# Three of the eight operations that decode a piece of weights go to ScalarE and GpSimd, the triangular solves are shared out anew, and the whole order is written again

## The chip, the cores and the metric

The kernel runs on one core of a Trainium2 chip. A core has a matrix engine (TensorE, PE in the profile, its weight loads PEld), a vector engine (VectorE, DVE), a scalar engine (ScalarE, ACT), GpSimd (POOL), and SyncE (SP), which here only issues DMAs. Each engine works through its own queue in order; semaphores tie the queues together. The metric is the device time of one launch in microseconds, as the median of several runs, in float32.

## The reference

A linear attention with decay and a delta rule runs over 768 time steps, for 4 batches and 8 heads of width 40. Its output, as 320 features for each token, goes through a gated feed-forward layer with a three-tap convolution along time.

```python
for t in range(S):
    y[:, :, t] = einsum('bhd,bhde->bhe', rt, state)
    Sa = einsum('bhde,bhe->bhd', state, at)
    state = state * wt[:, :, None, :] - einsum('bhd,bhe->bhde', Sa, bt) \
          + einsum('bhd,bhe->bhde', vt, kt)
# x = y, heads side by side: (4, 768, 320)
h = maximum(x @ w_in, 0)                       # 320 -> 1024
conv_out[s] = sum_k conv_w[k] * h[s + k - 1]   # along the tokens
return (h * sigmoid(conv_out)) @ w_out         # 1024 -> 320
```

The three weight arrays `w_in`, `conv_w` and `w_out` arrive as float64 and are read as pairs of 32-bit words. The kernel makes float32 numbers of them with integer and float operations (`from_f64`), and then a high and a low part of each, for products in several passes.

## The kernel before, in words

**Attention** goes in 24 steps of 32 tokens, two steps to a pair (12 pairs, `j` = 0 to 11). For a pair: `decays` (cumulated products of the decay, L365 to L381), `decayed` (a, k and b times these, L391 and L399), `scores` (`at`, L437: the products of the chunk), and from `at` the right-hand side `bb`, which goes through DRAM (`bd`) to bring one small triangular system to each partition (L461, L465). `solve` (L471 to L498) inverts them in 31 rounds of a multiply (L480) and an add (L486) and sends the result `xx` through DRAM (`xd`, L491) back to `tt` (L496). `VSOL` names the pairs whose solve is done by VectorE; the others are done by GpSimd. There is one buffer each for `xx`, `bb` and the temporary.

`chain` is the recurrence from step to step: `pp` on TensorE (L514, L522), its copy `psb` on ScalarE (L527), `pu` on TensorE from `psb` and `tt` (L533), its copy `u` (L538), the update `pn` on TensorE (L549), the addition of the old state on VectorE (`s`, L562), and its decay on GpSimd (`s`, L568), four instructions each for four batches. Both steps of a pair need `tt`, so steps 2j and 2j+1 can't end before solve j. Then `pairs`, `outputs` and `finish` give the 320 features of the step (`xf` L657, `xh` L665, `xl` L667).

**The feed-forward layer** goes in 12 windows of 64 tokens (two steps each): `moe_in` in four parts of 256 hidden columns (L700 to L743: products, relu, the taps L721 and L729, sigmoid L734, gating L736, split into high and low, L740 and L743), and `moe_out` in two halves (L754, L771).

**The weights** come in 23 pieces, 12 of `w_in` (`wi`), one of `conv_w` (`cv`) and 10 of `w_out` (`wo`, `wp`). A piece is a DMA, `from_f64` (eight VectorE operations of 128 x 256, L217 to L235), a cast to the high part on ScalarE (L253) and the low part on GpSimd (L255). The buffers of the pieces (tags `gh` and `gl`, four each) are those that the gated products of `moe_in` use later, so the first products wait for the last pieces.

**What sets the order.** Nothing is scheduled at run time: `ORDER` is a written list of tokens, such as `ch2*2`, and each token advances one generator to its next `yield`. Every instruction goes into its engine's queue in that order. A token that isn't ready in the sense of `put` first advances what it needs. Semaphores only make an engine wait at the head of its queue.

Of the kernel before, what the change touches and what calls it, by code (L numbers as in the profile page):

```python
# [8 lines left out]
F32 = mybir.dt.float32  # L9
# [11 lines left out]
VSOL = range(0, 12, 2)  # L21
# [13 lines left out]
    ld0 de0.0*2 ld0*2 de0.1 ld0 ld1 de0.1 we0 dd0.0*3 dd0.1*2 sc0 dd0.1 we0 ld1*2 lr0 sc0 sc1 lr1  # L35
    de1.0 sc1 ha0 de1.0 dd1.0 de1.1*2 we1*4 si0 ha0 ha1 dd1.0 we0*2 rt0 ld1 so0 ha1 dd1.0 so0 dd1.1
    ld2 so0*2 ld2 dd1.1 ld2 so0 dd1.1 ha2*2 sc2 ld2 lv0 lv1 vt0 ha3*2 so0*3 sc2 sc3 we2*2 sc3 we3
    we2*2 we3 we4 so0 we3*2 we5 we4 we5 si1 de2.0*2 ch0*4 we4*2 we6 lv2 de2.1*2 so1*2 ld3 ut0 pa0
    vt1 dd2.0*2 de3.0 we5 so1 we5 we7 ou0 we6 fi0 so1 dd2.0 ch1 we6 dd2.1 we7*2 ch1 we7 dd2.1*2 ld3
    st1*2 sc4 we6 so1 we8*4 we9 we10 ch1 lv3 rt1 we9 st1*2 ut1 pa1 lr2 ou1 ha4 ld3*2 we10 so1*3 fi0  # L40
    vt2 we10 fi0 fi1 de3.0 sc4 sc5 we9 we10 sc5 ch1 de3.1 we9 de3.1 ha4 we11 we12 lr3 rt2 fi1 st2*2
    fi1 we11 we12 we11*2 ro0 we13 we12*2 ha5 st2 we13 we14 ha5 ld4 so1 we13 dd3.0*3 dd3.1*3 we14*2
    ch2 si2 so2 ch2 pk0 ut2 so2*2 pa2 vt3 sc6 so2*2 st2 ou2 ch2 ro0 rt3 mi0.0*3 so2*2 mi0.0*2 ch2
    st3*2 we13 mi0.1*2 st3 ld4 so2 ld4 we14 lv4 we15 we16 ch3*2 sc6 sc7 ut3 we15 st3 we15 sc7 fi2*3
    lr4 mi0.0 pa3 mi0.0 ch3 we15 ch3 we16 mi0.0 we17 mi0.1 mi0.2 we17*2 mi0.2 so2 ch4 si3 we16 so3
    ou3 ha6 we16 we18 de4.0 we18 ha6 ha7 st4 fi3*2 we17 we19 de4.0 we18 mi0.1 we19 vt4 st4*3 lv5
    de4.1 ch4 ut4 so3 ch4 dd4.0 rt4 we18 we20 de4.1 we20 mi0.2 so3 we20 pa4 vt5 ch4 ch5 so3 mi0.2
    ch5 fi3 ha7 we19*2 we21*2 ut5 we20 we22*2 ou4 st5*2 mi0.1 st5 lr5 rt5 so3 we22 ld4 ld5 de5.0
    mi0.1 we21 ch5 we22 mi0.3 we21 mi0.0*2 so3 mi0.1*2 mi0.3 pa5 mi0.3 pk1 dd4.0*2 dd4.1 mi0.1*2
    dd4.1 st5 mi0.2 sc8 fi4*2 ld5 dd4.1 ou5 mi0.2 lv6 mi0.3 so3*2 sc8 mi0.2 sc9 mi0.2*2 ha8*2 ha9  # L50
    fi4 fi5 ld5 de5.0 de5.1 ha9 sc9 mi0.2 dd5.0 mi0.3 dd5.0 de5.1 lv7 mi1.0*3 mi1.1 ld5 dd5.0 dd5.1
    sc10 so3 si4 mi0.3 lr6 dd5.1*2 ch5 mi0.3 lr7 mi0.3 mi1.1*2 mi1.0*3 mi1.1 mi1.2 vt6 sc10 mi0.3
    mo0.0 sc11 mi0.3 mi1.1 mi1.0*2 mi1.1 ch6 st6 mi1.2 ch6*2 sc11 mi1.1*2 mo0.0*2 ch6 mo0.0 mo0.1*5
    ld6 ut6 rt6 ch7 mi1.1 so4 ld6 so4*2 pa6 vt7 st6 fi5*2 st6 so4*2 mi1.0 so4 mi1.2 st6 mi1.3 so4
    mi1.2 so4 lv8 ou6 mi1.0 mo1.0 mi1.2 mi1.3*2 st7*2 ch7 ut7 mi1.1 st7*2 rt7 ch7*2 mo1.0 pa7
    mi1.3*2 fi6*2 pk2 lr8 mi1.2*2 ou7 mi1.2 rt8 so4 si5 ch8 st8*2 mi1.2 mi1.3 mi1.2 mi1.3 ch8*2 lv9
    fi6 mi2.0*2 lr9 ld6 ch8 ha10*2 fi7 mi1.3*2 ha11 ld6 de6.0 vt8 lv10 de6.0 dd6.0 fi7 mi2.0 mi1.3
    mi2.1 ch9 mo1.0 mi2.0*2 de6.1 ch9 de6.1 so5*2 mi2.1 so5 mi2.0 ut8 mi2.1*4 mi2.0 mo0.0 mo1.0*2
    mo1.1 ha11 mi2.0 mi2.1 mo1.1 dd6.0 mo1.1 dd6.0 pa8 vt9 mo1.1 mi2.0*2 dd6.1 so5 fi7 st8*2 mi2.1*2
    dd6.1 so5 ou8 rt9 mi2.2 sc12 mi2.2*2 mi2.3*3 ut9 dd6.1 st9 mi2.1 mi2.2 ch9 mi2.2 mi2.3*2 mi2.2*2  # L60
    ld7 de7.0 lr10 ld7*2 so5*3 pa9 ch9 lr11 st9*3 pk3 ld7 mi2.3 mi2.2 mi3.0*2 mi2.3 mi3.0 mi2.3 fi8
    so5 fi8 mi2.2*2 mi2.3 mi3.0 ou9 mi3.1 fi8 sc12 fi9 de7.0 dd7.0 sc13 mo2.0*2 sc13 de7.1*2 mi3.1*2
# [940 lines left out]
```

## Time and profile before

| what | before |
|---|---|
| median of 3 runs | 708.97 us (708.5 to 709.71) |
| the profiled execution | 708.08 us, span 706.4 us |
| mean granted TensorE clock | 0.906 |
| TensorE busy | 560.7 us (79%) |
| VectorE busy | 538.4 us (76%) |
| ScalarE busy | 350.7 us (50%) |
| GpSimd busy | 353.2 us (50%) |

The profile is of one execution; its span, from the first to the last instruction, is 1.7 us shorter than its time. A row such as `L562 DVE TENSOR_TENSOR s<-pn,s 120x360 f32<-120x360 f32 x88 | 40.6, 522 | 20.6 <-PE pn L549 20.6` says: line 562 ran 88 times on VectorE with this shape, was busy 40.6 us in all, took 522 ns on the mean, and the engine had been idle 20.6 us before these, for the most part until L549 on TensorE was done. Busy time counts overlapping instructions once. In the rows of a timeline the first number is the start and the second the duration in microseconds, and xN is the number of instructions merged.

### The profile page before, as it was taken

Reading aid. Unit: us, or ns where it says so; the run is one execution under the profiler, and the core shown is the slowest. Engines: PE = TensorE matmul, PEld = TensorE weight load, DVE = VectorE, ACT = ScalarE, POOL = GpSimd, SP = SyncE. Lnnn points to the kernel's source line nnn. Section 1 sums busy time; section 2 is a strip of 40 time slices with the busy share of each in tenths; the row PEclk is TensorE's granted clock in tenths of the full one; section 3 lists DMA queues with packets and bytes.
Section 4 is the critical chain, followed back from the end, with each engine's and each line's share of the span. In section 5 each row is a group of like instructions: output and inputs, shape, how many; then the busy total and the mean of one; then the engine's idle time right before and its main releaser. Section 6 shows DMA issues by size and latency. Waiting matters only on the chain. (4 is left out here: it accounts for less than half of the span.)

```text
span 706.4 us, 29930 instructions
## 1 busy us (share of the span) xinstructions
PE 560.7 (79%) x13021; PEld 497.9 (70%) x13021; DVE 538.4 (76%) x1261; ACT 350.7 (50%) x792; POOL 353.2 (50%) x582
## 2 busy tenths in 40 slices
PE   4444764677687898988977996899998977899886
PEld 3334654566576787977866885789887876788775
DVE  6689889998999896657795578987979894456571
ACT  2322244254375455664454664466565546455651
POOL 2001884037786235783234884236985028863321
PEclk9766777997799998989999998999998999999998
DMA  8765456437125344544404446524435025121000
GB/s 139 120 117 108 103 112 102 95 94 144 22 41 107 56 72 79 94 81 82 82 20 89 86 86 106 81 60 69 89 62 91 6 54 94 29 51 32 21 30 19
DMA packets 242402, 53.40 MB, mean 76 GB/s; under 512 B 229000, under 2 KB 238112, under 8 KB 242272
## 3 DMA queue, kind: packets, MB, share of 16 engines
q1 hardware_dynamic: 242272, 51.50, 39.9%
q8 instruction: 102, 1.67, 1.0%
q14 instruction: 28, 0.23, 0.1%
HBM read 38.63 MB, written 10.22 MB: 69 GB/s over the span
## 5 line engine op out<-in xcount | busy, mean ns | idle before, releaser
L729 DVE SCALAR_TENSOR_TENSOR cc<-hb,cw,cc 128x256 f32<-128x256 f32 x192 | 106.3, 575 | 13.7 <-ACT cc L721 10.2
L568 POOL TENSOR_TENSOR s<-s,wc 120x360 f32<-120x360 f32 x88 | 75.8, 891 | 69.4 <-DVE s L562 69.4
L486 POOL TENSOR_TENSOR xx<-xx,st 128x126 f32<-128x126 f32 (+22 forms) x186 | 83.1, 447 | 14.6
L480 POOL TENSOR_TENSOR st<-xx,bb 128x126 f32<-128x126 f32 (+22 forms) x186 | 79.4, 427 | 21.1 <-DMA bb<-bd 8.4
L700 PE MATMUL ph<-xh,wih 120*128 120x256 f32 x288 | 56.6, 306 | 11.3 <-ACT hb L714 11.3
L486 DVE TENSOR_TENSOR xx<-xx,st 128x126 f32<-128x126 f32 (+22 forms) x186 | 54.2, 291 | 6.4
L480 DVE TENSOR_TENSOR st<-xx,bb 128x126 f32<-128x126 f32 (+22 forms) x186 | 53.6, 288 | 7.2 <-DMA bb<-bd 1.7
L736 DVE TENSOR_TENSOR cc<-cc,hb 128x512 f32<-128x512 f32 x48 | 40.8, 857 | 21.7 <-ACT cc L734 21.5
L562 DVE TENSOR_TENSOR s<-pn,s 120x360 f32<-120x360 f32 x88 | 40.6, 522 | 20.6 <-PE pn L549 20.6
L700 PEld LDWEIGHTS ph<-xh,wih 120*128 120x128 f32 x288 | 41.8, 194 | 15.0 <-ACT hb L714 13.1
L734 ACT ACTIVATE cc<-cc 128x512 f32<-128x512 f32 x48 | 30.4, 636 | 43.6 <-DVE cc L729 43.5
L667 POOL TENSOR_TENSOR xl<-xf,xh 120x384 fp32r<-120x384 f32 x24 | 26.8, 1117 | 45.2 <-ACT xh L665 41.5
L721 ACT ACTIVATE cc<-hb,cw 128x256 f32<-128x256 f32 x96 | 43.5, 506 | 8.7 <-DVE hb L712 2.9
L602 PE MATMUL pt<-ident,s 120*120 120x120 f32 x276 | 40.6, 279 | 6.4 <-DVE s L562 3.2
L427 ACT ACTIVATE ap<-ah,hmask 120x384 f32<-120x384 f32 (+1 forms) x72 | 36.6, 576 | 17.4 <-DVE ah L391 10.1
L604 ACT COPY sn<-pt 120x360 f32<-120x360 f32 x92 | 38.9, 471 | 12.2 <-PE pt L602 11.8
L714 ACT ACTIVATE hb<-ph 128x512 f32<-128x512 f32 x48 | 28.8, 600 | 27.2 <-PE ph L700 23.4
L579 ACT ACTIVATE rp<-pr,hmask 120x384 f32<-120x384 f32 x72 | 36.7, 586 | 6.9 <-PE pr L576 6.5
L700 PE MATMUL ph<-xl,wih 120*128 120x256 f32 x192 | 39.3, 287 | 0.0
L533 PE MATMUL pu<-psb,tt 32*32 32x40 f32 x1536 | 22.5, 209 | 19.6 <-ACT psb L527 16.1
L602 PEld LDWEIGHTS pt<-ident,s 120*120 120x120 f32 x276 | 31.2, 143 | 9.0 <-DVE s L562 3.5
L533 PEld LDWEIGHTS pu<-psb,tt 32*32 32x32 f32 x1536 | 18.7, 114 | 24.5 <-ACT psb L527 17.7
(867 smaller groups left out, 1665.9 us busy)
## 6 DMA issues: line engine op xcount, KB each, us to landing
bb<-bd SPq DMA_DIRECT2D x24, 256.0 KB
w<-in_w_dram SPq DMA_DIRECT2D x24, 160.0 KB
a<-in_a_dram SPq DMA_DIRECT2D x24, 160.0 KB
k<-in_k_dram SPq DMA_DIRECT2D x24, 160.0 KB
b<-in_b_dram SPq DMA_DIRECT2D x24, 160.0 KB
r<-in_r_dram SPq DMA_DIRECT2D x96, 40.0 KB
v<-in_v_dram SPq DMA_DIRECT2D x96, 40.0 KB
out_dram<-ob SPq DMA_DIRECT2D x22, 160.0 KB
```

The lines of the kernel that those rows point to most:

```text
L480: eng.tensor_tensor(t3, xx[:, 0:nj, i : i + 1].to_broadcast([128, nj, nt]), bb[:, i : i + 1, i + 1 :].to_broadcast([128, nj, nt]), ALU.mult,)
L486: eng.tensor_tensor(xx[:, 0:nj, i + 1 :], xx[:, 0:nj, i + 1 :], t3, ALU.add)
L533: nc.tensor.matmul(pu[quad(bi), hc], tt[quad(bi), c, h, :], psb[quad(bi), hc], start=(h == 0), stop=True, skip_group_check=True,)
L562: nc.vector.tensor_tensor(new, pn[bi][:GR], old[bi], ALU.add)
L568: nc.gpsimd.tensor_tensor(n4, n4, w4, ALU.mult)
L579: nc.scalar.activation(out=rp[:, :, h, :], in_=pr[:GR], func=AF.Copy, scale=hmask[:, h : h + 1])
L602: nc.tensor.transpose(pt[:GR, g, :], old[bi][:, g, :], ident[:GR, :GR])
L604: nc.scalar.copy(sn, pt[:GR])
L700: nc.tensor.matmul(ph[:, j], l[:, fs], x, start=(j == 0 and i == 0), stop=(i == len(passes) - 1), skip_group_check=True,)
L721: nc.scalar.activation(out=cc[:, j], in_=hb[:, j, :, 1 : W + 1], func=AF.Copy, scale=cw[:, 1, f : f + 1],)
L729: nc.vector.scalar_tensor_tensor(out=cc[:, j], in0=hb[:, j, :, x : W + x], scalar=cw[:, x, f : f + 1], in1=cc[:, j], op0=ALU.mult, op1=ALU ...
L736: nc.vector.tensor_tensor(cc, cc, hb[:, :, :, 1 : W + 1], ALU.mult)
```

## The change

`from_f64` computes one float32 from two words: `t` and `e` (exponent and high bits), `m` (the high bits of the low word, as an integer), then `tf` (the main part or zero), `ef` (a power of two) and `tf + m * 2**-44 * ef`. Before, all eight operations are VectorE's. Now the scale of `m` and its conversion to float is an ACTIVATE on ScalarE, and the product with `ef` and the last sum are GpSimd's; VectorE keeps six. `VSOL` was 0, 2, 4, 6, 8, 10 and is 0, 3, 5, 7, 9, 11: both engines still do six solves each, but solves 1 and 2 are now both GpSimd's, and the last one, 11, is VectorE's. `ORDER` is written anew from end to end.

```diff
-VSOL = range(0, 12, 2)
+VSOL = (0, 3, 5, 7, 9, 11)
...
         tf, ef = t.bitcast(F32), e.bitcast(F32)
+        nc.scalar.activation(out=m.bitcast(F32), in_=m, func=AF.Copy, scale=2.0**-44)
         V.scalar_tensor_tensor(out=tf, in0=e, scalar=896.5, in1=tf, op0=ALU.is_ge, op1=ALU.mult)
         V.tensor_scalar(out=e, in0=t, scalar1=-(1 << 23), scalar2=None, op0=ALU.bitwise_and)
-        V.scalar_tensor_tensor(
-            out=ef, in0=m, scalar=2.0**-44, in1=ef, op0=ALU.mult, op1=ALU.mult
-        )
-        V.tensor_tensor(tf, tf, ef, ALU.add)
+        nc.gpsimd.tensor_tensor(ef, m.bitcast(F32), ef, ALU.mult)
+        nc.gpsimd.tensor_tensor(tf, tf, ef, ALU.add)
         return tf
...
 ORDER (the rows around the second solve, of some 70 rows that all differ)
-    fi1 we11 we12 we11*2 ro0 we13 we12*2 ha5 st2 we13 we14 ha5 ld4 so1 we13 dd3.0*3 dd3.1*3 we14*2
-    ch2 si2 so2 ch2 pk0 ut2 so2*2 pa2 vt3 sc6 so2*2 st2 ou2 ch2 ro0 rt3 mi0.0*3 so2*2 mi0.0*2 ch2
+    we11*2 we13*2 so1 ch2*2 ro0 we12 si2 ch2 de3.1*2 st2*2 ut2 ch2 so2 lv3 lv4 pa2 st2*2 ou2 vt3 ch3
+    rt3 ch3 dd3.0 so2 dd3.1*2 ro0 fi2*2 st3 sc6 pk0 mi0.0 we13 mi0.0 so2 mi0.0 mi0.1*4 dd3.1 ch3 ut3
```

The changed file has one line less behind L217, so lines from the middle of `from_f64` on carry other numbers there: L231 and L232 are the old L230 and L231, L230 is the new ScalarE operation, L233 and L234 are GpSimd's two, and everything behind is one lower (L561 is the old L562, L567 the old L568, L472, L479 and L485 the old L473, L480 and L486). The queues at three places:

**VectorE at a piece of weights** (`wi01`, the fourth; `r` is its raw words, `q` and `s` the work buffers). Before:

```order
L217 TENSOR_SCALAR wi01q<-wi01r 120x256
L221 TENSOR_SCALAR wi01q<-wi01r 120x256
L225 SCALAR_TENSOR_TENSOR wi01q<-wi01r,wi01q 120x256
L228 TENSOR_SCALAR wi01s<-wi01r 120x256
L230 SCALAR_TENSOR_TENSOR wi01q<-wi01q 120x256
L231 TENSOR_SCALAR wi01q<-wi01q 120x256
L232 SCALAR_TENSOR_TENSOR wi01q<-wi01s,wi01q 120x256
L235 TENSOR_TENSOR wi01q<-wi01q 120x256
```

Now, on VectorE:

```order
L217 TENSOR_SCALAR wi01q<-wi01r 120x256
L221 TENSOR_SCALAR wi01q<-wi01r 120x256
L225 SCALAR_TENSOR_TENSOR wi01q<-wi01r,wi01q 120x256
L228 TENSOR_SCALAR wi01s<-wi01r 120x256
L231 SCALAR_TENSOR_TENSOR wi01q<-wi01q 120x256
L232 TENSOR_SCALAR wi01q<-wi01q 120x256
```

The last two rows are gone from VectorE's queue; GpSimd has two more ahead of the one it had.

**GpSimd behind the second solve** (`s` with four buffers is the decay of the state in step 2 of the chain; `xx`, `st` and `bb` belong to a solve). Before:

```order
L255 TENSOR_TENSOR wil<-wi23q,wih 120x256
L710 MEMSET hb_2023 128x8x2
L568 TENSOR_TENSOR s_1993<-s_1993,wc_259 120x360
L568 TENSOR_TENSOR s_1995<-s_1995,wc_259 120x360
L568 TENSOR_TENSOR s_1997<-s_1997,wc_259 120x360
L568 TENSOR_TENSOR s_1999<-s_1999,wc_259 120x360
L255 TENSOR_TENSOR wol<-wo0q,woh 128x256
```

Now:

```order
L254 TENSOR_TENSOR wil<-wi23q,wih 120x256
L233 TENSOR_TENSOR wo0q<-wo0s,wo0q 128x256
L234 TENSOR_TENSOR wo0q<-wo0q 128x256
L567 TENSOR_TENSOR s_1739<-s_1739,wc_250 120x360
L567 TENSOR_TENSOR s_1741<-s_1741,wc_250 120x360
L567 TENSOR_TENSOR s_1743<-s_1743,wc_250 120x360
L567 TENSOR_TENSOR s_1745<-s_1745,wc_250 120x360
L472 CAST xx_1782<-xini 128x512
L479 TENSOR_TENSOR st_0_1784<-xx_1782,bb_1708 128x31
L485 TENSOR_TENSOR xx_1782<-xx_1782,st_0_1784 128x31
```

Solve 2 now stands in GpSimd's queue, right behind the decay of step 2.

**VectorE at the state of step 2** (`s` from `pn`). Before, in the midst of solve 2:

```order
L480 TENSOR_TENSOR st_19_1877<-xx_1736,bb_1733 128x120
L486 TENSOR_TENSOR xx_1736<-xx_1736,st_19_1877 128x10x12
L562 TENSOR_TENSOR s_1993<-pn_1965,s_1218 120x360
L562 TENSOR_TENSOR s_1995<-pn_1966,s_1220 120x360
L562 TENSOR_TENSOR s_1997<-pn_1967,s_1222 120x360
L562 TENSOR_TENSOR s_1999<-pn_1968,s_1224 120x360
L480 TENSOR_TENSOR st_20_2034<-xx_1736,bb_1733 128x121
```

Now:

```order
L231 SCALAR_TENSOR_TENSOR wo0q<-wo0q 128x256
L232 TENSOR_SCALAR wo0q<-wo0q 128x256
L561 TENSOR_TENSOR s_1739<-pn_1711,s_1129 120x360
L561 TENSOR_TENSOR s_1741<-pn_1712,s_1131 120x360
L561 TENSOR_TENSOR s_1743<-pn_1713,s_1133 120x360
L561 TENSOR_TENSOR s_1745<-pn_1714,s_1135 120x360
L368 SCALAR_TENSOR_TENSOR suf_1753<-wx_107,dsuf 120x384
```

The additions of step 2 now stand right behind the piece `wo0`, with no solve ahead of them but solve 0.

More of the change, by code (lines that the diff above doesn't have):

```diff
@@ L45 @@
[L45 to L50, printed above, removed]
@@ L102 @@
[L102 to L105 removed]
+    ld0*2 de0.0*2 dd0.0 de0.1*2 ld0 dd0.0 ld0 dd0.0 we0 we1 dd0.1 sc0 dd0.1*2 we0 sc0 ld1*3 de1.0*2
+    lr0 sc1 ha0*2 ha1*2 de1.1 ld1 sc1 dd1.0*2 ld2 de1.1 si0 dd1.0 dd1.1 ld2 dd1.1 sc2 dd1.1 ha2*2
@@ new lines @@
+    fi16 mi6.2 fi16 mi6.3*2 mi7.1*2 si10 lr19 mi6.3 mi7.0 vt18 fi17 ch18 ld11 mi7.0 fi17 ld11 de11.0
+    fi17 mo6.0 mi7.1*2 ch18 mo6.0 mo6.1 lr20 mi7.0*2 mi7.1 mi7.0 ch18 ha20 ha21 mo6.1 so10 mi7.1
+    mi7.2*3 mo6.1*2 mi7.0 mi7.1*2 st18 ut18 mo6.0 lv20 mi7.2 mi7.0 so10 mi7.1*2 so10 mi7.3*2 ha21
+    de11.1 ch19*2 de11.1 so10 mi7.2*2 mi7.3 mo6.1 st18*3 mo7.0 dd11.0 mi7.2*2 mi7.3*2 pa18 mi7.2
+    ch19 ou18 rt19 st19*2 pk8 st19*2 mi7.3*2 ut19 mi7.3*2 mi8.0 mo7.0 mi8.0*2 vt19 mi8.0 mi7.2
+    mi8.0*2 mi8.1*3 so10 pa19 vt20 mi7.3 mi8.1 so10 dd11.0*2 mi8.1 dd11.1*2 fi18 sc22 mo7.0*2 ou19
```

124 lines of the change are left out of this document (61 added, 63 removed).

## The prediction, made before the changed kernel had run

> **What bounds the kernel now.** I read the busy shares and the slices first, then the stretches, then the waits, and the chain that ended last at the end.
>
> ```profile
> PE 560.7 (79%) x13021; PEld 497.9 (70%) x13021; DVE 538.4 (76%) x1261; ACT 350.7 (50%) x792; POOL 353.2 (50%) x582
> PE   4444764677687898988977996899998977899886
> DVE  6689889998999896657795578987979894456571
> POOL 2001884037786235783234884236985028863321
> ```
>
> No engine is the bound throughout. A slice is 17.7 us. VectorE has 8 and 9 for most of the first 14 slices, TensorE only from the thirteenth on. The stretches say the same in microseconds:
>
> ```profile
> core 0: us, PE busy (x) PEld busy (x) DVE busy (x) ACT busy (x) POOL busy (x), PEclk, DMA share, GB/s
> 0.00:200.00 200.00, 120.79 (x2866) 103.19 (x2867) 172.44 (x442) 72.35 (x168) 85.12 (x164) 0.79 0.54 102
> 240.00:580.00 340.00, 301.60 (x7318) 270.36 (x7316) 267.56 (x626) 188.65 (x428) 181.42 (x283) 0.95 0.41 73
> 580.00:640.00 60.00, 51.62 (x1242) 46.45 (x1242) 27.35 (x56) 34.87 (x78) 44.18 (x81) 0.97 0.29 56
> ```
>
> To 200 us VectorE is busy 172.4 us (86%) and TensorE 60%; from 240 to 580 TensorE is busy 89% and VectorE 79%. So the front is VectorE's and the rest TensorE's. The front matters only in so far as TensorE's work behind it starts earlier. The chain that ended last holds 20 us of the last window and tells nothing of the front. The waits add this:
>
> ```profile
> POOL s L568 <- DVE s L562: 69.4, 13, 23.4
> DVE s L562 <- PE pn L549: 20.6, 11, 4.6
> ```
>
> GpSimd waits long for the recurrence (69.4 us, once 23.4), while VectorE waits little for TensorE (20.6 us): VectorE always has something else ahead.
>
> **What VectorE loses.** Two of eight operations in each of 23 pieces, 46 in all (the third, the multiplication by 2**-44, was part of one of them).
>
> ```profile
> 55.59 0.43 DVE L232 SCALAR_TENSOR_TENSOR wi20q<-wi20s,wi20q 120x256 f32<-120x256 int32 x1
> 56.05 0.42 DVE L235 TENSOR_TENSOR wi20q<-wi20q 120x256 f32<-120x256 f32 x1
> 56.39 0.68 DVE L437 TENSOR_TENSOR at<-ps,trin 128x512 f32<-128x512 f32 x1
> ...
> 196.57 0.54 DVE L235 TENSOR_TENSOR wp1q<-wp1q 128x256 f32<-128x256 f32 x1
> ```
>
> From the start of the first to the start of what follows is 56.39 - 55.59 = 0.80 us, or 23 x 0.80 = 18.4 us. This pair had GpSimd idle beside it. With some pairs slower I take 0.85, so 19.5 us, all within the front: the last row is the end of the last piece.
>
> **What GpSimd and ScalarE gain.** The nearest rows are their own operations on the same tile:
>
> ```profile
> L255 POOL TENSOR_TENSOR wil<-wi00q,wih x1: 725/725/725, 31.8 to 31.8; 120x256 fp32r<-120x256 f32 x1
> ...
> L255 POOL TENSOR_TENSOR wil<-wi01q,wih x1: 932/932/932, 60.8 to 60.8; 120x256 fp32r<-120x256 f32 x1
> L255 POOL TENSOR_TENSOR wil<-wi11q,wih x1: 890/890/890, 64.0 to 64.0; 120x256 fp32r<-120x256 f32 x1
> L253 ACT CAST wih<-wi20q x1: 404/404/404, 56.5 to 56.5; 120x256 fp32r<-120x256 f32 x1
> ```
>
> GpSimd gets 46 operations of 0.73 to 0.93 us in that view; at 0.8 that is 37 us, and with its 85.1 us it would be busy 122 of 200. ScalarE gets 23 x 0.40 = 9.3 us on 72.3 of 200. I cost ScalarE's at nothing: it is idle 128 us there, and the copies behind these are for the same pieces; without that cover it is at most the 9.3 us.
>
> More GpSimd time slows VectorE:
>
> ```profile
> L228 DVE TENSOR_SCALAR wi00s<-wi00r x1: 286/286/286, 15.8 to 15.8; 120x256 int32<-120x256 int32 x1
> L228 DVE TENSOR_SCALAR wi11s<-wi11r x1: 815/815/815, 61.0 to 61.0; 120x256 int32<-120x256 int32 x1
> L399 DVE TENSOR_TENSOR kt<-pk,suf x24: 539/546/558, 12.7 to 549.6; 120x384 f32<-120x384 f32 x24
> L729 DVE SCALAR_TENSOR_TENSOR cc<-hb,cw,cc x192: 469/485/1493, 153.7 to 688.6; 128x256 f32<-128x256 f32 x192
> L729 DVE SCALAR_TENSOR_TENSOR cc<-hb,cw,cc 128x256 f32<-128x256 f32 x192 | 106.3, 575 | 13.7 <-ACT cc L721 10.2
> ```
>
> One and the same operation takes 286 ns with GpSimd idle and 815 beside one of its subtractions. L399, which reads one operand from PSUM, never changes (539 to 558). Bounds: nothing (as L399), or 0.53 us for each new GpSimd operation, 46 x 0.53 = 24 us, more than the whole saving. L729 lies between: its mean is 575 against a least of 469, so 192 x 0.106 = 20 us, over the 353.2 us that GpSimd is busy, 0.06 us each. It is a third of the lines that behave so; I take 0.15, nearer to L729 than to L228 since most of what runs beside is not L228, and get 37 x 0.15 = 5.5 us. VectorE's net relief is then 19.5 - 5.5 = 14 us.
>
> On this the Trainium skill (GPSIMD Engine Reference, section 8, Key points) says that GpSimd shares its SBUF interfaces with VectorE and contends with its instructions in a two-port mode or with two SBUF inputs. The trace agrees with both halves (815 ns; L399 unmoved). Taken for every new operation it gives the upper bound, and no gain at all.
>
> **What the share-out of the solves does.** Solve 1 stays on GpSimd; solve 2 now waits behind it. These rows of before give its steps:
>
> ```profile
> 71.08 0.24 POOL L480 TENSOR_TENSOR st<-xx,bb 128x31 f32<-128x31 f32 x1 [5.59 <-DMA bb<-bd]
> 104.96 0.77 POOL L486 TENSOR_TENSOR xx<-xx,st 128x16 f32<-128x16 f32 x1
> 108.43 1.93 SPq L491 DMA_DIRECT2D xd<-xx  x2
> 112.67 1.73 SPq L496 DMA_DIRECT2D tt<-xd  x4
> 127.81 0.79 PE L533 MATMUL pu<-psb,tt 32*32 32x40 f32 x64 [2.77 <-ACT psb L527]
> 140.31 3.15 POOL L568 TENSOR_TENSOR s<-s,wc 120x360 f32<-120x360 f32 x4 [23.37 <-DVE s L562]
> 180.08 3.71 POOL L568 TENSOR_TENSOR s<-s,wc 120x360 f32<-120x360 f32 x4 [0.26 <-DVE s L562]
> 235.63 3.51 POOL L568 TENSOR_TENSOR s<-s,wc 120x360 f32<-120x360 f32 x4 [5.96 <-DVE s L562]
> ```
>
> The last three rows are the decays of steps 2, 4 and 6. Solve 1's input (`at`, the row at 56.39) is now behind two more pieces, each shorter by 0.8: about 2 us later, so the solve starts at 73 instead of 71.1. It took 34.7 us (71.08 to 105.73) with four subtractions within; now two pairs, two lone operations and 2 us more: it ends near 110. From there to the end of the last `tt` issue was 8.7 us; 2.3 for a transfer (112.67 less the end of `xd`, 110.36), and some 5 for `pu`, `u`, `pn` and the additions: the decay of step 2 starts near 126. Before, 140.3: **a lead of 14 us**, because VectorE no longer sits in solve 2 when `pn` is ready.
>
> VectorE itself reaches these additions earlier than that. Between the last `at` and them stand nine pieces at six operations and the preparation of three half-pairs, 45 us by the means of their lines, so it is there about 105 to 108 and idles some 15 us. That is late next: in the front the chain, not VectorE, now sets the pace, and solve 2 stands behind step 2's decay on GpSimd. For a solve on each engine:
>
> ```profile
> 591.93 0.24 POOL L480 TENSOR_TENSOR st<-xx,bb 128x31 f32<-128x31 f32 x1
> 623.98 0.24 POOL L486 TENSOR_TENSOR xx<-xx,st 128x16 f32<-128x16 f32 x1
> 344.99 0.19 DVE L480 TENSOR_TENSOR st<-xx,bb 128x31 f32<-128x31 f32 x1
> 365.66 0.19 DVE L486 TENSOR_TENSOR xx<-xx,st 128x16 f32<-128x16 f32 x1
> ```
>
> GpSimd takes 32.3 us, VectorE 20.9. Solve 2: 126 + 3.2 + 0.7 = 130, end 162 or a little less, and 8.7 + 2.3 + 5 = 16 to step 4's decay: 177 to 178 against 180.1, **a lead of 2.5**. Solve 3 is next on VectorE behind step 4's additions, 20.9 us and some 7 of other work between: 205, and 16 more, 221 against 235.6 for step 6, **a lead of 14**. The mean of the three is 10, within VectorE's net relief of 14. I take 11 (step 4's is small because the new order asks more of TensorE ahead of it). TensorE's instructions are the same in number, so at an unchanged density what leads at 240 leads at the end.
>
> **The last solve.** Moved to VectorE it ends 32.3 - 20.9 = 11 us sooner. From 580 to 640 TensorE is busy 86% against 88.7% from 240 on: 60 x 0.027 = 1.6 us is what it could win. I take 2.
>
> **Sum.** The profiled execution took 708.1 us (span 706.4). 708.1 - 11 - 2 = 695.1. The median of the runs is 0.9 above the profiled one, so the forecast is **696 us**.
>
> **Rivals.**
>
> *All of the relief and a denser TensorE.* After 240 VectorE is busy 79%, and TensorE idles 38.4 of 340 us, much of it in short gaps behind other engines. If the order drawn anew closes a third of that (13) and the front gives the upper 19.5, it is 709 - 19.5 - 13 = 676. For it: slices 8 to 9 on both engines from 340 to 580. Against it: the solves are as many on VectorE as before.
>
> *The lead is given back.* TensorE's queue is rewritten, and where it is 89% busy a new order can as well cost 10 us as win them. Then 708 to 710, no change. For it: the even spread of TensorE's small waits; against: nothing shows that the old order was the better one.
>
> *GpSimd becomes the bound of the front (slower).* Solves 1 and 2, the 46 operations and the decays all stand in one queue between 73 and 180. How long a solve can get there, another row shows:
>
> ```profile
> 165.63 0.24 POOL L480 TENSOR_TENSOR st<-xx,bb 128x31 f32<-128x31 f32 x1 [1.10 <-DMA bb<-bd]
> 215.58 0.23 POOL L486 TENSOR_TENSOR xx<-xx,st 128x16 f32<-128x16 f32 x1
> ```
>
> Solve 3 took 50 us with pieces, a decay and waits between. At 50 each instead of 36 and 32, step 4 comes 14 + 18 = 32 us later than I reckon, 210 against 180. Of these 30 us VectorE's relief gives 14 back afterwards: 709 + 16 = 725. It decides as soon as the two solves together take over 71 us. For it: GpSimd is the slower engine for this work (890 ns for what took VectorE 420). Against: GpSimd was idle over half of the front, and solve 2 now runs without pieces between.
>
> The Trainium skill (GPSIMD Engine Reference, section 4.1, Engine selection) advises against this change: elementwise work belongs on VectorE, GpSimd being about twice as slow with two inputs. The rows agree (890 to 420), and by that rule alone this rival would be the outcome.
>
> **Chances and range.** Forecast 0.46, its own range 687 to 704. Denser TensorE 0.22, given back 0.10, GpSimd as the bound 0.22. The range for 8 in 10 is 672 to 718: it takes in the fast rival and the nearer part of the slow one, whose full bound, contention's 24 us in place of 5.5, would come to the same 715 to 725. Faster by over 0.2% (which is about what a measurement here can tell, 1.4 us): 0.69; within it: 0.09; slower: 0.22.
>
> **What would show it.** Right: VectorE busy falls by 10 to 17 us in all, GpSimd rises by 32 to 45; the decays of steps 2, 4 and 6 start near 126, 178 and 221; VectorE waits some 15 us for `pn` of step 2; the last piece is decoded 10 to 20 us before 197. Wrong: VectorE's sum falls by less than 5 (contention), step 4 later than 185 (GpSimd's queue), or a lead at step 6 that isn't there at the end (TensorE's order).

## The result, and the profile after

| kernel | time, us (median, least to most) | ratio to before, 95% interval |
|---|---|---|
| before, same chip | 709.3 (708.5 to 710.2) | 1 |
| after | **746.1** (744.3 to 747.1) | **1.0516** (1.0490 to 1.0542) |

The change makes the kernel 37 us slower. The forecast was 696, with 672 to 718 as its range: wrong in sign and outside the range. The profiled execution of the changed kernel has a span of 745.4 us (before 706.4), so 39.0 us are to be found. First the busy shares and slices of the changed kernel, a slice being 18.6 us now:

```profile
PE 564.5 (76%) x13021; PEld 503.1 (67%) x13021; DVE 529.3 (71%) x1215; ACT 357.7 (48%) x815; POOL 381.5 (51%) x628
PE   4413663894569887987987978888979898889886
DVE  6899348479998648755778876466897757886651
POOL 2117776787555784213885226781226866223311
```

VectorE's row no longer has 8 and 9 throughout the front: its fifth to ninth slices have 3, 4, 8, 4, 7. Nothing took its place. The stretches of the changed kernel, those that the prediction shows of before:

```profile
core 0: us, PE busy (x) PEld busy (x) DVE busy (x) ACT busy (x) POOL busy (x), PEclk, DMA share, GB/s
0.00:200.00 200.00, 106.92 (x2562) 90.75 (x2563) 145.12 (x339) 74.36 (x178) 116.72 (x223) 0.79 0.57 105
240.00:580.00 340.00, 284.39 (x6725) 256.64 (x6723) 242.13 (x560) 178.54 (x406) 177.78 (x291) 0.93 0.42 73
580.00:640.00 60.00, 52.64 (x1254) 48.15 (x1255) 41.45 (x86) 34.53 (x78) 38.36 (x66) 0.94 0.23 44
```

To 200 us VectorE is busy 145 us in place of 172, TensorE 107 in place of 121, GpSimd 117 (forecast 122). VectorE is still the fullest engine there, at 73%, and no other is busy for over 60% of the time: they wait for one another. The waits of the changed kernel (time waited in all, times, longest):

```profile
POOL s L567 <- DVE s L561: 64.7, 12, 16.2
PE pu L532 <- ACT psb L526: 47.1, 13, 28.6
DVE s L561 <- PE pn L548: 35.2, 13, 5.2
```

VectorE now waits 35.2 us for TensorE's `pn` (20.6 before). The longest wait of TensorE, 28.6 us, is for `psb` of step 0.

**Where the 39 us lie.** The same four stretches of both kernels, first before, then after:

```profile
0.00:240.00 240.00, 153.13 (x3601) 131.81 (x3602) 208.00 (x508) 94.69 (x217) 110.05 (x202) 0.82 0.53 99
240.00:480.00 240.00, 209.35 (x5182) 187.18 (x5181) 181.58 (x438) 132.31 (x301) 120.73 (x190) 0.94 0.44 77
480.00:640.00 160.00, 143.88 (x3380) 129.63 (x3378) 113.32 (x244) 91.20 (x204) 104.88 (x174) 0.97 0.32 60
640.00:760.00 120.00, 54.33 (x865) 49.30 (x863) 35.51 (x74) 32.52 (x70) 17.56 (x16) 0.96 0.05 13
```

```profile
0.00:240.00 240.00, 138.10 (x3449) 117.17 (x3450) 181.04 (x425) 93.18 (x222) 135.84 (x246) 0.79 0.51 95
240.00:480.00 240.00, 199.44 (x4809) 179.53 (x4808) 167.24 (x387) 124.54 (x282) 130.25 (x215) 0.93 0.41 72
480.00:640.00 160.00, 137.60 (x3173) 125.26 (x3172) 116.33 (x261) 88.52 (x200) 85.89 (x142) 0.94 0.36 63
640.00:760.00 120.00, 89.39 (x1598) 81.14 (x1597) 64.67 (x146) 51.50 (x113) 29.55 (x27) 0.91 0.12 27
```

TensorE's idle time is the length of a stretch less its busy time. To 240 us it goes from 86.9 to 101.9 (15.0 more), from 240 to 480 from 30.7 to 40.6 (9.9), from 480 to 640 from 16.1 to 22.4 (6.3), and behind 640, up to the spans' ends, from 12.1 to 16.0 (3.9). The same 13021 matmuls take 3.8 us longer (564.5 against 560.7), though in decay_ahead, the changed kernel but for one token, they take 559.1. These five make 38.9. So less than half of the loss is in the front, where the prediction looked; the rest comes where not one operation was moved.

### The profile page after: what moved, and what is told of

Same layout as the page of the kernel before. It is cut to its first block, busy times and chain, and to the rows that moved or that the text cites. A ratio compares the mean times of both kernels' runs of the same rounds, so it can differ in the third digit from the quotient of the medians.

```text
span 745.4 us, 29993 instructions
## 1 busy us (share of the span) xinstructions
PE 564.5 (76%) x13021; PEld 503.1 (67%) x13021; DVE 529.3 (71%) x1215; ACT 357.7 (48%) x815; POOL 381.5 (51%) x628
## 5 line engine op out<-in xcount | busy, mean ns | idle before, releaser
L728 DVE SCALAR_TENSOR_TENSOR cc<-hb,cw,cc 128x256 f32<-128x256 f32 x192 | 109.4, 590 | 12.4 <-ACT cc L720 8.9
L567 POOL TENSOR_TENSOR s<-s,wc 120x360 f32<-120x360 f32 x88 | 76.9, 904 | 64.7 <-DVE s L561 64.7
L485 POOL TENSOR_TENSOR xx<-xx,st 128x126 f32<-128x126 f32 (+22 forms) x186 | 77.8, 418 | 14.6
L479 POOL TENSOR_TENSOR st<-xx,bb 128x126 f32<-128x126 f32 (+22 forms) x186 | 77.1, 415 | 14.0 <-DMA bb<-bd 0.8
L699 PE MATMUL ph<-xh,wih 120*128 120x256 f32 x288 | 59.7, 319 | 20.3 <-ACT hb L713 20.3
L479 DVE TENSOR_TENSOR st<-xx,bb 128x126 f32<-128x126 f32 (+22 forms) x186 | 59.5, 320 | 10.9 <-DMA bb<-bd 5.1
L561 DVE TENSOR_TENSOR s<-pn,s 120x360 f32<-120x360 f32 x88 | 40.6, 523 | 35.7 <-PE pn L548 35.2
L735 DVE TENSOR_TENSOR cc<-cc,hb 128x512 f32<-128x512 f32 x48 | 36.6, 765 | 35.8 <-ACT cc L733 35.6
L485 DVE TENSOR_TENSOR xx<-xx,st 128x126 f32<-128x126 f32 (+22 forms) x186 | 56.6, 304 | 6.4
L699 PEld LDWEIGHTS ph<-xh,wih 120*128 120x128 f32 x288 | 44.3, 205 | 24.5 <-ACT hb L713 22.8
L601 PE MATMUL pt<-ident,s 120*120 120x120 f32 x276 | 43.7, 293 | 1.8 <-DVE cc L728 1.1
L601 PEld LDWEIGHTS pt<-ident,s 120*120 120x120 f32 x276 | 33.9, 151 | 4.2 <-issue 1.4
```

Of the source, the lines that this page charges most:

```text
L479: eng.tensor_tensor(t3, xx[:, 0:nj, i : i + 1].to_broadcast([128, nj, nt]), bb[:, i : i + 1, i + 1 :].to_broadcast([128, nj, nt]), ALU.mult,)
L485: eng.tensor_tensor(xx[:, 0:nj, i + 1 :], xx[:, 0:nj, i + 1 :], t3, ALU.add)
L561: nc.vector.tensor_tensor(new, pn[bi][:GR], old[bi], ALU.add)
L567: nc.gpsimd.tensor_tensor(n4, n4, w4, ALU.mult)
L601: nc.tensor.transpose(pt[:GR, g, :], old[bi][:, g, :], ident[:GR, :GR])
L699: nc.tensor.matmul(ph[:, j], l[:, fs], x, start=(j == 0 and i == 0), stop=(i == len(passes) - 1), skip_group_check=True,)
```

## The experiments

The theories at the start: **queues** (the moved operations hold up what stands behind them), **order** (the new list of tokens and the new shares cost the time, the move does not), **contention** (GpSimd slows VectorE). Medians of one kernel differ by up to 3 us between chips, so ratios go to before on the same chip. The four short kernels ran once each, on two chips, so a few us between them are not safe.

| run | what it is | us | ratio to before (95%) |
|---|---|---|---|
| moved_only | old list, old shares, operations moved | 734.5 | 1.0337 (1.0291 to 1.0384) |
| shares_only | old list, new shares | 814.1 | 1.1453 (1.1395 to 1.1512) |
| old_order | old list, new shares, moved | 832.3 | 1.1711 (1.1656 to 1.1765) |
| new_order_shares | new list, new shares, nothing moved | 739.0 | 1.0391 (1.0336 to 1.0445) |
| part_moved | before, ten pieces of 23 moved | 710.9 | 1.0022 (0.9989 to 1.0056) |
| decay_ahead | after, one token earlier | 748.4 | 1.0516 (1.0469 to 1.0563) |
| before_short | before, 30 of 31 solve rounds left out | 683.9 | one run |
| after_short | after, the same | 721.5 | one run |
| order_short | new list and shares, nothing moved, the same | 701.5 | one run |
| old_front_short | lists joined at step 7, the same | 715.8 | one run |
| new_front | new list to step 7, then old | 734.3 | 1.0333 (1.0269 to 1.0396) |
| old_front | old list to step 7, then new | 745.2 | 1.0488 (1.0423 to 1.0552) |
| after_inplace | after, one work buffer less a piece | 741.8 | 1.0444 (1.0388 to 1.0500) |
| before_inplace | before, the same | 709.6 | 0.9982 (0.9941 to 1.0023) |
| moved_only_inplace | moved_only, the same | 735.3 | 1.0348 (1.0309 to 1.0387) |
| after_scale_dve | after, scale of `m` on VectorE | 741.8 | 1.0437 (1.0397 to 1.0477) |
| scale_only | new list and shares, only the scale moved | 749.2 | 1.0569 (1.0525 to 1.0612) |
| after_again | after, beside scale_only | 742.9 | 1.0475 (1.0434 to 1.0517) |

### One part of the change at a time

**Only the move** (`from_f64` as after, the rest as before):

```diff
+        nc.scalar.activation(out=m.bitcast(F32), in_=m, func=AF.Copy, scale=2.0**-44)
...
-        V.scalar_tensor_tensor(
-            out=ef, in0=m, scalar=2.0**-44, in1=ef, op0=ALU.mult, op1=ALU.mult
-        )
-        V.tensor_tensor(tf, tf, ef, ALU.add)
+        nc.gpsimd.tensor_tensor(ef, m.bitcast(F32), ef, ALU.mult)
+        nc.gpsimd.tensor_tensor(tf, tf, ef, ALU.add)
```

> The order and the shares of before, with only the three operations of each weight piece on ScalarE and GpSimd. Theory 'queues' (the moved operations themselves do the harm: the scale stands at the head of ScalarE's queue, the product and the sum at that of GpSimd's, and what is behind them, psb of step 0 and solve 1, waits): 725 us or more, with solve 1 on GpSimd longer than 40 us and TensorE idle near 50 us as in the changed kernel. Theory 'order' (the new list of tokens and the new shares do the harm): 697 to 712, VectorE some 10 us less busy, and the decays of steps 2 and 4 no later than before (140 and 180). Theory 'contention' (GpSimd slows VectorE): 712 to 725 with VectorE's sum down by less than 5.

734.5: the move alone costs 25 us in the old order. VectorE's sum fell to 525.8 us, so the operations did leave it, and yet the kernel is slower. The timeline of GpSimd in that run, the first and last row of solve 1 and two rows in its midst:

```profile
70.02 0.24 POOL L479 TENSOR_TENSOR st<-xx,bb 128x31 f32<-128x31 f32 x1 [1.27 <-DMA bb<-bd]
...
100.57 0.73 POOL L233 TENSOR_TENSOR wi03q<-wi03s,wi03q 120x256 f32<-120x256 f32 x1 [1.38 <-ACT wi03s L230]
...
107.73 0.74 POOL L233 TENSOR_TENSOR wi13q<-wi13s,wi13q 120x256 f32<-120x256 f32 x1 [5.62 <-ACT wi13s L230]
...
120.85 0.23 POOL L485 TENSOR_TENSOR xx<-xx,st 128x16 f32<-128x16 f32 x1
```

The solve takes 51.1 us in place of 34.7. GpSimd stands at the product of `wi13` for 5.62 us, since ScalarE has not scaled its operand, and the solve's rounds stand behind. (VectorE has `m` ready at 104.5; ScalarE scales it at 107.2, behind a copy that waits 4.6 us for TensorE.) The other four pieces in its midst take GpSimd's time as well. Step 2 is 14 us late from then on, and solve 3, with the products of five pieces in it, takes 62 us in place of 50.

**Only the shares, the list undone, and the move undone:**

```diff
-VSOL = range(0, 12, 2)
+VSOL = (0, 3, 5, 7, 9, 11)
```

> The order and the decoding of before, with the solves shared out as in the changed kernel (0, 3, 5, 7, 9, 11 on VectorE). Nothing of the order moves, each solve's instructions only go to the other engine's queue. Theory 'order', in the form that two solves one behind the other on GpSimd delay steps 4 and 5: 720 to 740, step 4's decay near 200 in place of 180. Theory 'queues': 705 to 715, since GpSimd has no decoding but the low parts in front of them.

> The moved operations and the new shares, in the order of before: only the list of tokens is undone. If the new list itself costs the time, 700 to 715; if the moved operations and the shares cost it together, 735 to 755 as in the changed kernel (746). In between, the list is part of it, by the difference to 746.

> The changed kernel with the eight operations of a piece back on VectorE: the new order and shares without the move. Theory 'queues': 705 to 720, that is most of the 37 us come back, and TensorE is busy some 8 us between 40 and 60 as before. Theory 'order': 745 to 765, since VectorE gets 19.5 us of work back in the front and nothing of the order is better.

The shares alone cost 104 us and with the move 123: the old list can't be used with the new shares (the decay of step 2 sits in the midst of solve 2 on GpSimd and starts at 151, not 140, and so it goes on, pair by pair). The new list was written for them, and takes most of that back. No run has the new list with the old shares, so the two count as one here. But with nothing moved it is still at 739.0, 29 us above before. Of the 37 us the new list with its shares so costs about 29, the move the rest. The theory "order" has the larger part, yet not in its form that the move does no harm. TensorE's long wait for `psb` of step 0 is the list's too: 26.7 us with nothing moved.

### What the move costs

**Move only where GpSimd has no solve to do:**

```diff
+MOVED = ("wi00", "wi10", "wi20", "wi01", "wi11", "wi21", "wi23", "wo0", "wo1", "wo2")
...
-    def from_f64(raw, e, t, m):
+    def from_f64(raw, e, t, m, mv=False):    # the new form if mv, else the old one
```

> The kernel before, its order and shares, with the three operations moved in ten of the 23 pieces only, those that are decoded while GpSimd has no solve to do (wi00, wi10, wi20, wi01, wi11, wi21 ahead of solve 1; wi23, wo0, wo1, wo2 between solves 1 and 3). With all pieces moved it took 734.5, and solve 1 took 51 us in place of 35, with GpSimd waiting at wi03 and wi13 in its midst. Theory 'solve behind a piece' (a solve on GpSimd waits at the head of the queue for the operands of a moved product): the 25 us go away, solve 1 takes 34 to 37 us and the time is 698 to 711; ten pieces free 8 us of VectorE, so a gain of up to 8 is possible. Theory 'contention or handing over' (each moved piece costs its share, wherever it stands): 25 x 10/23 = 11 us, 718 to 722.

710.9, the same as before. Solve 1 in that run, its first and last row:

```profile
70.66 0.24 POOL L487 TENSOR_TENSOR st<-xx,bb 128x31 f32<-128x31 f32 x1 [1.40 <-DMA bb<-bd]
...
104.74 0.23 POOL L493 TENSOR_TENSOR xx<-xx,st 128x16 f32<-128x16 f32 x1
```

34.3 us again. In the old order, then, the 25 us come with the 13 pieces that are not moved here, ten of them in the midst of solves 1 and 3, and "each piece costs its share" (718 to 722) falls. The run shows a second thing: ten pieces less two operations leave VectorE 5.8 us less busy to 240 us, and none of it is gained. Its waits to 200 us grew instead (for TensorE, at `at` from 3.1 to 6.3 and at `ah` from 1.6 to 3.9). By these waits VectorE was the fullest engine of the front and still not what paced it. The run does not prove it alone: the same edit gives ScalarE ten operations and GpSimd twenty, whose cost may have taken a gain back.

**Buffers held longer.** From its first operation to its low part a piece takes 13.6 us in the changed kernel and 11.6 with nothing moved, on the mean of the 22 that have a low part, and it holds two of the four buffers of the tag `gl` meanwhile.

```diff
-        q2 = gp.tile([128, 512], F32R, tag="gl", name=nm + "s").bitcast(I32)
-        return t, q[:, 0:256], q[:, 256:512], q2[:, 0:256]
+        return t, q[:, 0:256], q[:, 256:512], t.rearrange("p (c z) -> p c z", z=2)[..., 0]
```

> The changed kernel, with the third work array of a piece (m) kept in the place of the low words that it is made from, so that a piece holds one buffer of the tag gl in place of two and twice as many pieces can be under way. In the changed kernel a piece takes 13.4 us from its first operation to its low part, with the old decoding under the same list 11.2. Theory 'longer hold' (the moved operations cost 7 us because the pieces hold their buffers longer and the next ones wait): 737 to 742. If the buffers do not matter: 744 to 749.

> The control: the same edit in the kernel before. VectorE writes and reads m with a stride, some 0.1 us more a piece at most. Every theory: 705 to 713, since VectorE, not the buffers, sets the pace of its pieces.

> The old list and shares with all pieces moved (734.5) and the same edit. Here solve 1 on GpSimd waited 5.6 us at the product of wi13, and wi13 itself began 5 us later than before. Theory 'longer hold': wi13 begins at 98 again, solve 1 takes 40 us or less, 715 to 726. Theory 'solve behind a piece' alone (the product stands in the midst of the solve and waits for ScalarE's scale, however many buffers there are): 730 to 736.

The control is unmoved (709.6). moved_only stays at 735.3, and `wi13` begins at 103.7 as without the edit (103.4). after_inplace came to 741.8, inside the range of this theory, but its profiled pieces begin no earlier (`wi03` 103.7 against 102.1), and the changed kernel itself came to 742.9 on another chip. The theory falls.

**ScalarE's scale, taken back, and moved alone:**

```diff
-        nc.scalar.activation(out=m.bitcast(F32), in_=m, func=AF.Copy, scale=2.0**-44)
+        V.tensor_scalar(out=m.bitcast(F32), in0=m, scalar1=2.0**-44, scalar2=None, op0=ALU.mult)
```

> The changed kernel with the scale of m taken back from ScalarE to VectorE as an operation of its own; the product and the sum stay on GpSimd. VectorE gets 23 operations of about 0.3 us (7 us), ScalarE loses 9.3. Theory 'ScalarE's queue' (the scale waits at its head and holds up psb and the copies behind it): 737 to 742, the wait for psb of step 0 shorter than 28.6 us. Theory 'GpSimd only': 745 to 750.

```diff
-        nc.gpsimd.tensor_tensor(ef, m.bitcast(F32), ef, ALU.mult)
-        nc.gpsimd.tensor_tensor(tf, tf, ef, ALU.add)
+        V.tensor_tensor(ef, m.bitcast(F32), ef, ALU.mult)
+        V.tensor_tensor(tf, tf, ef, ALU.add)
```

> The changed kernel with the product and the sum back on VectorE; only the scale of m stays on ScalarE. It is the complement of the run with the scale taken back (741.8, 1.0437 of before, against 1.0516 for the changed kernel and 1.0391 with nothing moved). If ScalarE's operation is what costs the 7 us, this one stays at 744 to 748 (1.049 to 1.054). If GpSimd's two cost them, 737 to 742 (1.037 to 1.045).

> The changed kernel itself beside it, since 5 us can only be told on one and the same chip: 744 to 748, ratio 1.049 to 1.054 as in its first runs. If it comes out under 742 here, the 7 us between it and the run with nothing moved are not safe either.

With the scale on VectorE 741.8, with only the scale on ScalarE 749.2. The wait for `psb` of step 0 did not get shorter (29.6 us), so that part of the theory was wrong. The 741.8 (1.0437) is no clear gain on the changed kernel either, which came to 1.0475 when run again. Against nothing moved (1.0391) the scale alone costs 1.8% (1.0569, the intervals apart), 10 to 13 us; GpSimd's two operations then give 6 us back (1.0475 on the same chip). The waits of ScalarE in scale_only, from 40 to 215 us:

```profile
ACT wi20s L230 <- DVE wi20s L228: 18.5, 1, 18.5
ACT wi22s L230 <- DVE wi22s L228: 8.6, 1, 8.6
ACT wo7s L230 <- DVE wo7s L228: 6.5, 1, 6.5
ACT wi23s L230 <- DVE wi23s L228: 5.8, 1, 5.8
```

The scale stands at the head of ScalarE's queue until VectorE has made `m`. Not every such wait is a cost. With nothing moved, the cast of `wi20` waits there as long:

```profile
ACT wih L253 <- DVE wi20q L235: 19.8, 1, 19.8
```

What the scale adds is more such places (26 waits for pieces in this stretch, 73.8 us, against 11 and 53.8), and one of them is right in front of `psb` of step 2. In scale_only, then with nothing moved:

```profile
129.56 0.42 ACT L230 ACTIVATE wo0s<-wo0s 128x256 f32<-128x256 int32 x1 [2.10 <-DVE wo0s L228]
129.88 0.42 ACT L526 ACTIVATE psb<-pp 128x320 f32<-128x320 f32 x1
```

```profile
123.91 0.41 ACT L253 CAST wih<-wi23q 120x256 fp32r<-120x256 f32 x1 [8.27 <-DVE wi23q L235]
124.22 0.43 ACT L527 ACTIVATE psb<-pp 128x320 f32<-128x320 f32 x1
```

`pp` is done at 124.3 and at 122.8, so `psb` starts 5.6 us behind it with the scale and 1.4 without. Step 2's decay is then 4.9 us later, and those of steps 5 to 22 are 6 to 10 us later. No run moved the scale of `wo0` alone, so its part in the 10 us is read from these rows and not measured. The Trainium skill (PSUM — Partial Sum Buffer, section "Engine vs sequencer instructions") says that the queues of ScalarE, VectorE and GpSimd are strictly first in, first out; these rows and the 5.62 us above agree.

The changed kernel beside scale_only came to 742.9, just over the top of what was written for an unsafe difference (under 742). Against nothing moved (739.0, 1.0391) its excess is 4 us here and 7 in the first runs by the medians, 6 and 9 by the ratios. The interval here overlaps with that of nothing moved, that of the first runs does not. The net cost of the move under the new list is a few microseconds, no more can be said.

### What the new list costs

**A decay in front of the solve.** Of the three steps forecast, step 4 is the first late one (steps 1 and 3, for which nothing was forecast, come 10 and 14 us later than before), and in the changed kernel the decay of step 3 stands behind solve 2.

```diff
-    mi0.0*3 so2*2 st3*3 mi0.1 sc6 sc7 we12 we14 so2*3 ld4 ...
-    ... ha6*2 ha7*2 mi0.1 fi3 ld4*2 ch3 mi0.1 de4.0 ...
+    mi0.0*3 ch3 so2*2 st3*3 mi0.1 sc6 sc7 we12 we14 so2*3 ld4 ...
+    ... ha6*2 ha7*2 mi0.1 fi3 ld4*2 mi0.1 de4.0 ...
```

> The changed kernel with one token moved: the decay of step 3 goes ahead of the last rounds of solve 2 in GpSimd's queue. In the changed kernel step 3's additions end at 156, but its decay starts at 172, behind solve 2, and psb of step 4 is ready at 183. Theory 'decay behind the solve': the decay starts near 157, psb of step 4 near 170, solve 2 ends 3 us later (170), u of step 4 is then set by tt and comes at 181 in place of 185; of these 4 us what reaches the end shows whether the front still sets it: 741 to 744. Theory 'the front does not set the end': 745 to 748.

748.4, no gain. The decay went from 171.6 to 152.5, and `psb` of step 4 from 183 to 186. A miss: the decay was not what `psb` waited for. The timelines of the changed kernel, of TensorE and then ScalarE, show what was:

```profile
176.33 1.08 PE L410 MATMUL ps<-ap,kt 120*32 120x96 f32 x24 [7.12 <-ACT ap L426]
177.18 1.08 PE L410 MATMUL ps<-ap,bt 120*32 120x96 f32 x24
178.04 1.29 PE L513 MATMUL pp<-s,ah 120*32 120x120 f32 x24
```

```profile
174.76 1.52 ACT L426 ACTIVATE ap<-ah,hmask 120x256 f32<-120x256 f32 x3 [4.55 <-DVE ah L390]
...
182.71 0.40 ACT L252 CAST woh<-wo3q 128x256 fp32r<-128x256 f32 x1 [1.75 <-POOL wo3q L234]
183.02 0.43 ACT L526 ACTIVATE psb<-pp 128x320 f32<-128x320 f32 x1
```

`pp` of step 4 is queued behind `ps`, the scores of step 8, and these wait 7 us for an `ap` that waits for `ah` on VectorE. Then `psb` stands behind the cast of `wo3`, which waits for GpSimd's sum. The new list has the work of later steps, and pieces, in front of the step that is due.

**Without the solves.** One round of 31 is done, in both kernels and with the new list alone:

```diff
         for i in range(C - 1):
             if i in cuts:
                 yield
+            if i >= 1:
+                continue
```

> The kernel before with one of the 31 rounds of every solve, 30 left out: what the kernel takes when the solves cost next to nothing and tt is there early. VectorE loses some 120 us of 538, GpSimd some 200 of 353; TensorE's 560 are unchanged, so not under 600. If the solves pace the steps, 640 to 680; if TensorE's own queue does, 695 to 709.

> The changed kernel with the same 30 of 31 rounds left out of every solve. Theory 'solves' (the 37 us come from where and when the solves are done): the two short kernels are within 10 us of one another. Theory 'rest of the order' (TensorE's and the other queues' own order, without the solves): the changed one stays 25 to 40 us above the other. In between: each has its part.

> The new list and shares, the decoding of before, 30 of 31 rounds left out of every solve: with the two short kernels before (683.9 for the old list, 721.5 for the changed kernel) it parts the list from the moved operations where no solve is in the way. If the moved operations cost only by holding up solves, 717 to 722 (they cost nothing here); if they cost by themselves as in the full kernels (7), 712 to 716.

683.9, 721.5 and 701.5. The difference between the two kernels stays whole, 37.6 us: "where and when the solves are done" is not the cause, though in the full kernels the solves have a part. With nothing moved 17.6 remain: the list's own. The other 20 come with the moved operations, which have no solve to hold up here; the expectation had them at nothing or at 7. Of these 20 only 7.4 are idle time of TensorE. The stretch from 240 to 480, of before_short and then of order_short:

```profile
240.00:480.00 240.00, 215.96 (x5370) 194.13 (x5365) 144.68 (x292) 139.52 (x316) 77.75 (x81) 0.97 0.46 80
```

```profile
240.00:480.00 240.00, 199.71 (x4762) 180.52 (x4763) 134.48 (x272) 128.75 (x291) 68.00 (x69) 0.94 0.41 73
```

TensorE idles 40.3 us in place of 24.0, and that is nearly all of the list's loss: in the other stretches the two differ by under 1 us each. TensorE's waits there, of before_short and of order_short:

```profile
PE ph L702 <- ACT hb L716: 7.4, 5, 3.7
PE pu L535 <- ACT psb L529: 0.7, 2, 0.5
```

```profile
PE ph L702 <- ACT hb L716: 14.3, 7, 5.4
PE pu L535 <- ACT psb L529: 2.7, 3, 1.2
PE ps L411 <- ACT ap L427: 2.1, 3, 1.2
PE pm L411 <- ACT rp L581: 1.6, 1, 1.6
```

All rows of that view in which TensorE waits for a copy of ScalarE add up to 12.0 us before and 26.7 with the new list, 14.7 of the 16.3. The full kernels show the same in this stretch: 14.6 before, 28.0 with nothing moved, 27.5 in the changed one. The new list puts TensorE's next product close behind the copy that it reads, where the old one had other work between. This is read from the traces; no run moved these tokens alone.

**Half a list each.** The lists were joined behind the decay of step 7, each token done once, nothing moved.

```diff
-ORDER = the old list
+ORDER = the new list to the last ch7, then the old one without what is done   # new_front; VSOL (0, 3, 4, 6, 8, 10)
+ORDER = the old list to the last ch7, then the new one without what is done   # old_front; VSOL (0, 2, 5, 7, 9, 11)
```

> The decoding of before. The new list of tokens up to the decay of step 7 (some 265 us), and from there the old list, less what has been issued; solves 0, 3, 4, 6, 8, 10 on VectorE, so that each part keeps its own shares. With the old decoding the old list takes 709.6 and the new one 739.0. Theory 'rest' (the loss comes from the list behind step 7, where the kernel with one round a solve lost 15 of its 19 us of TensorE's time): 709 to 718. Theory 'front' (what is lost by step 7 stays, and more): 730 to 742. If both lose: near 724.

> The other half of the exchange: the old list up to the decay of step 7, then the new one, the old decoding, solves 0, 2, 5, 7, 9, 11 on VectorE. Theory 'rest': 728 to 740. Theory 'front': 709 to 716. The two mixed lists have a seam that neither had, with some work at another place than planned, so a few us on both are no evidence.

> The old list up to the decay of step 7, then the new one, the old decoding, one of 31 rounds of every solve. Theory 'rest': 705 to 722, most of the 34 to 38 us between the short kernels. Theory 'front': 684 to 695.

734.3, 745.2 and 715.8, against 739.0 for the whole new list (701.5 in the short form). Both halves lose, and the joined list with the old front is slower than the whole new one, in both forms. The seam costs as much as what was to be told apart, so these three decide nothing.

## Why the prediction was wrong, point by point

The sum took 11 us for leads in the front and 2 for the last solve. The 11 are what failed, by the steps below. As to the 2: the last solve did take 23.3 us on VectorE in place of 32.3 on GpSimd, but TensorE's idle time behind 640 us grew by 3.9, so nothing of it was won.

**Prices: right, but for contention.** A piece that nothing disturbs keeps VectorE 1.8 us in place of 2.7 (0.85 was taken off), and GpSimd's new operations take 0.72 to 0.98 in most rows (0.8). GpSimd was busy 117 us to 200 (forecast 122), and its sum rose by 28.3 (32 to 45 written). VectorE's sum fell by 9.1 (10 to 17 written), and 2.5 of that came with the list: with nothing moved it is 535.9, in the changed kernel 529.3. So the net relief was 6.6 where 14 was reckoned, and by one profile of each the deduction for contention should have been some 13 (19.5 less 6.6) and not 5.5. It did not decide the time, since VectorE was then idle for 55 of the first 200 us.

**"So the front is VectorE's": the first step that failed.** VectorE's 86% was read as the bound of the front, and its net relief, 14 us, as time to be gained; the leads only had to fit within it. part_moved takes 5.8 us off and gains nothing, though it isn't a pure test. By the waits the chain from step to step and the solve paced the front, and VectorE's work filled the time beside them.

**ScalarE's operations "at nothing": the second.** The cover named was that ScalarE idles 128 of 200 us and that the copies behind are for the same pieces; the bound without cover was 9.3 us. The scale alone measured 10 to 13. ScalarE's idle time was no cover, since the scale waits at the head of its queue for VectorE, and what stands behind is not only for the same piece: in the changed kernel, too, `psb` of step 2 stands right behind the scale of `wo0`, which waits 3.6 us, and starts at 128.0 (124.2 with nothing moved).

**The leads of 14, 2.5 and 14: wrong from step 4 on.** The rows of GpSimd's decays of steps 2, 4 and 6, and of solve 2, in the changed kernel:

```profile
132.95 3.71 POOL L567 TENSOR_TENSOR s<-s,wc 120x360 f32<-120x360 f32 x4 [3.00 <-DVE s L561]
...
137.96 0.24 POOL L479 TENSOR_TENSOR st<-xx,bb 128x31 f32<-128x31 f32 x1
...
167.12 0.23 POOL L485 TENSOR_TENSOR xx<-xx,st 128x16 f32<-128x16 f32 x1
...
197.04 0.73 POOL L233 TENSOR_TENSOR wo7q<-wo7s,wo7q 128x256 f32<-128x256 f32 x1 [2.20 <-ACT ut L592]
197.84 0.73 POOL L234 TENSOR_TENSOR wo7q<-wo7q 128x256 f32<-128x256 f32 x1
198.53 3.10 POOL L567 TENSOR_TENSOR s<-s,wc 120x360 f32<-120x360 f32 x4
...
239.75 3.71 POOL L567 TENSOR_TENSOR s<-s,wc 120x360 f32<-120x360 f32 x4
```

Step 2 came at 133 (126 forecast, 140 before): a lead, of 7; VectorE waited 4 us for its `pn`, not 15. Solve 2 took 29.4 us, less than the 32 reckoned. What failed is "8.7 + 2.3 + 5 = 16 to step 4's decay": it took 31 (167.4 to 198.5), because `pp` stood behind the scores of step 8, `psb` behind a cast, the additions, whose `pn` was done at 187.1, behind pieces on VectorE until 190.7, and the decay itself, whose additions were done at 192.5, behind the moved operations of `wo7` on GpSimd until 198.5. The last 6 us are the move's: with nothing moved this decay starts 0.9 us behind its additions. The 8.7 and 2.3 were measured at solve 1 of the old list and the 5 was estimated; none of them allows for waits in queues such as these four. Step 4 later than 185 was written as the sign of GpSimd's queue, and that queue has 6 of the 20 us. Step 6 came at 240 (221 forecast, 236 before). Solve 3 took 34 us on VectorE, with the last pieces in it, where 20.9 and some 7 of other work were reckoned.

**"The last piece is decoded 10 to 20 us before 197":** it came at 213 on VectorE, 214.5 with GpSimd's sum. VectorE was half idle from 80 to 160 us (busy 43 of 80), but `wo1` stands so far back in the list that it began at 159.8 (124.3 before).

**"At an unchanged density what leads at 240 leads at the end":** failed twice. There was no lead at 240, and the density fell: TensorE idled 16.2 us more from 240 to 640. The prediction had this as the rival "the lead is given back", with 10 us as the price and 0.10 as the chance. It named the right place; the price (16 us for the list in the short form) and the chance were too small.

**The rival on the other side** (GpSimd the bound, 725) had the sign right and the place, but for the 6 us at step 4, wrong. It was to decide when solves 1 and 2 take over 71 us together; they took 36 and 29. GpSimd's two operations even gave 6 us under the new list. Under the old list, in the midst of the solves, the same operations cost 25 with the scale. The Trainium skill (GPSIMD Engine Reference, section 4.1, Engine selection) advises elementwise work on VectorE and not on GpSimd; the 25 us agree with that, the 6 do not.

**What stays open.** Why the moved operations cost 20 us in the short kernels and only 4 to 9 in the full ones (12.7 of the 20 are TensorE's busy time, 567.0 us at a clock of 0.884 against 554.3 at 0.915, in one run each), and which single places of the new list cost its 16 us in the middle.

## What to carry to other kernels

Where engines work through queues written out by hand, a busy share of 86% does not by itself make an engine the bound: take a few microseconds off it in a place where nothing else changes, and see whether the end moves, before pricing a larger relief. An operation handed to an idle engine whose operand is late holds up whatever is queued behind it there, so look at what stands next in that queue, and not at the idle share: ten pieces moved outside the solves left the time as it was, all 23 cost 25 us. And a list written anew is a change of its own, to be timed without the change that it was written for: here it was most of the loss.

## What the runs showed of the hardware

Where TensorE was idle the most, the same work also took it longer. The busy line of old_order, and its span and mean granted clock:

```profile
PE 586.9 (71%) x13021; PEld 518.5 (62%) x13021; DVE 508.1 (61%) x1215; ACT 359.7 (43%) x815; POOL 361.9 (44%) x628
```

```profile
core 0: 830.7 us, clock 0.852
```

The same 13021 matmuls take 586.9 us there, with 244 us of idle time, and 583.4 at a clock of 0.859 in shares_only, with 228. Before it was 560.7 at 0.906, with 146. The Trainium skill (TensorE: Matmul & The Clock Gate, Part 1: The HAM clock gate) has the throttled clock as the default and activity as what releases it; these two runs agree in direction. In the other 18 profiles TensorE idles for 128 to 189 us, and there its busy time, from 553.7 to 567.0 us, does not follow: after_short has 567.0 at 0.884 with 153 us of idle time, after_scale_dve 553.7 at 0.903 with 184. So the 3.8 us of the changed kernel can't be put down to its idle time; in old_order, with 26 us, it is likely.
